# The odd keys' copy on another DMA queue in two parts, a new order of key tiles, and a higher floor of filler products

## The chip, the cores and the metric

The kernel runs on one core of one Trainium2 chip. The metric is the device time of one launch in microseconds (us). The kernel before was run five times: 739.42, 739.61, 740.66, 749.91 and 750.74 us, with a median of 740.66 us. One more execution was recorded by the hardware profiler, and all durations below come from it.

The engines are named as the profile names them: PE (TensorE, matmuls; PEld are its weight loads), DVE (VectorE), ACT (ScalarE), POOL (GpSimd) and SP (SyncE, which here only issues DMAs).

## The reference

The result is a gated sum of two branches that read the same 2048 x 512 input `x`. Branch A is attention with 32 query heads of 16 elements and a single key and value head. Branch B is a gated MLP with a spatial product over the 2048 positions.

```
g = sigmoid(sum(x * gate_w))                      # one gate per position
q = x @ wq -> 32 heads x 2048 x 16 ; k = x @ wk ; v = x @ wv   # k, v: 2048 x 16
a = softmax(q k^T / 4) v  -> 2048 x 512, then @ wo
z = gelu(x @ w_in) ; z1, z2 = halves (688 columns each) ; z2 = layernorm(z2)
b = (z1 * (w_sp @ z2 + b_sp)) @ w_out
out = g * a + (1 - g) * b
```

The scores are 32 x 2048 x 2048 numbers, and each goes through an exponential. That is most of the work.

## The kernel before

**Tiles.** The scores are cut into 32 units. A unit is one of four stretches of 512 queries and one of eight slots; each slot holds four heads, one in each of the four 32-row groups of PE. Odd and even units share a query tile: rows 0 to 15 of a 32-row group belong to the even unit's head and rows 16 to 31 to the odd one's. The key tile `KA` therefore exists twice. `KA[:, 0]` has the keys in the even rows, written by DVE from a PE result (the keys' evacuation, L355), one copy for each of the four stretches of 512 keys. `KA[:, 1]` has the same keys in the odd rows; it is filled by four DMAs from `KA[:, 0]`, one for each row group (`k_shift`, L357), because the move goes from one partition to another. Before the change these four are issued by POOL once all four stretches of keys are there.

A unit has 16 key tiles (128 keys each) by 4 row groups, which makes 64 blocks of 128 x 512 scores. The order in which a unit takes its key tiles is the list `KL` (L35). ACT takes blocks from the front of the list, two to an instruction: an exponential from two PSUM banks to the buffer `P` (L631). DVE takes key tiles from the back of the list, at most seven in a unit, as batches of four blocks. It replaces the exponential by the square of a squared linear term: an instruction on 1024 columns for each pair of blocks (L655), a square over 2048 (L667), and a last square, a part of which goes to POOL (L667 and L674). What the polynomial leaves out is corrected for each unit by two more products with the tables `MC` and `CC`, built once from the keys (`Kt`) and values of the last seven entries of `KL` (`g_MC`, L455). `Kt` holds those keys, repeated, one column block for each key tile. In the old list the last seven entries are all the third or fourth key tile of their stretch, and `Kt` keeps exactly those two of each stretch.

PE makes the scores (`s_mm`, L618), the products of weights and values ("P,V" and "X,V" in the profile), and, between them, everything else: keys, values, queries, branch B and the output projections. At the start a queue of groups has to go in order (L756): values of stretch 0, keys 1, keys 2, values 1, keys 3, values 2, values 3, the correction tables and so on. They share one PSUM bank, `BM`.

**The planner.** The order of instructions on each engine is not written by hand. While the program is built, a list scheduler plays PE, ACT and DVE against a table of assumed durations, and appends an instruction to an engine's program whenever that engine is free and a candidate is ready. On the chip each engine then runs its own list in order and waits on semaphores. What is due to be ready is kept in a table `T`. `T["K1"]` (L367) is the time from which odd units may start; before the change it is the planned end of the last keys' evacuation plus 4500 ns. No score of an odd unit, for ACT or for DVE, is planned before that. A DVE batch of the unit in progress is opened only while the unit has at least 32 blocks left between the two ends (L811).

**Unread products.** `keep_pick` (L1057) adds matmuls that nobody reads. The planner sums the planned load of PE over the last 3400 ns, where a matmul over the full 128 x 128 array and 512 columns counts as 1, so that a score or value product with a 32-row or 32-column tile counts as 0.25. If the sum is below `KEEP` a filler is offered: ones times ones into `BM` when that bank is idle, or zeros added to the bank of running sums `BO` when all four sums of a unit are open. While the sum is also below `LOW`, its priority is 1.5, ahead of value products (2) and of the groups for `BM` (3); between `LOW` and `KEEP` it is 9, behind all that is ready. A candidate that would end past the deadline for the next pair of score blocks for ACT is dropped, fillers included.

**The queues.** SP issues, in this order: the four transposing loads of `x`, the loads of `w_in` (two), `b_sp`, `wo`, `w_out` (three), then four transposing loads of the first quarter of `w_sp` (`ld_wT(0)`, L304). Later quarters and the outputs follow on the same queue. ACT issues the small loads and `wq` before its first activation.

The expression of `keep_pick` that decides:

```
have = sum(w_ for _, w_ in load)
if have >= KEEP or st_["pu"] >= NU:
    return None
...
return (now, 1.5 if have < LOW else 9, C512 + sw("M"), emit, None, "M")
```

Of the kernel before, what the change touches and what calls it, by code (L numbers as in the profile page):

```python
# [15 lines left out]
S = 2048  # L16
D = 512
DH = 16
# [13 lines left out]
ZMAX = 25.0  # L32


KL = (0, 1, 2, 4, 5, 8, 9, 12, 13, 6, 10, 14, 15, 11, 7, 3)  # L35

NPB = 21
NX = 6
# [2 lines left out]
NMAX = 7  # L41
# [16 lines left out]
SLATE = 535.0  # L58
FREE = 60.0
SEEN = 204.0  # L60
KEEP = 7.5
LOW = 6.5
MMARG = 120.0
PMARG = 200.0
PRE = 12
# [107 lines left out]
def build_kernel(nc, x_d, wq_d, wk_d, wv_d, wo_d, win_d, wsp_d, bsp_d, wout_d, gw_d, out_d):  # L173
    es = ExitStack()
    with es:
# [24 lines left out]
        KA = sb("KA", [128, 2, S], B16)  # L200
        QA = sb("QA", [128, NQ, 512], B16)
        V1 = sb("V1", [128, NKT, 32], B16)
        KT0 = sb("KT0", [128, NKT, DH], B16)
        Kt = sb("Kt", [128, 8, 128], B16)
# [18 lines left out]
        ones = sb("ones", [128, 512], B16)  # L223
# [30 lines left out]
        op = pg.op  # L254
# [18 lines left out]
        def dma(eng, fn, r=(), w=(), n=16, tag="", after=()):  # L273
            return op(eng, fn, r=r, w=w, dma=n, tag=tag, after=after)
# [23 lines left out]
        def ld_wT(tc):  # L298
            prev = []
            for k in range(4):  # L300
                r0 = 512 * tc + 128 * k
                prev = [dma("sp", lambda q, r0=r0, k=k: q.dma_start_transpose(wT[:, :, 128 * k:128 * k + 128], wsp_d[r0:r0 + 128, :]),
                            w=[("wT", k)], tag="wT", after=prev)]
        ld_wT(0)  # L304

        for g in range(4):
            op("dve", lambda v, g=g: v.tensor_scalar(wk_rep[:, :, 32 * g:32 * g + 16], wk_sb[:], 0.25, None, ALU.mult), r=["wk"], w=["wk_rep"])
# [38 lines left out]
        def setT(k):  # L346
            def f(t):
                T[k] = t
            return f
# [4 lines left out]
        def k_ev(c, b):  # L354
            op("dve", lambda v: v.tensor_copy(KA[:, 0, 512 * c:512 * c + 512], bank(b)), r=[bkey(b)], w=[("K", 0, c)], tag="Kev")  # L355

        def k_shift():  # L357
            for g in range(4):
                dma("pool", lambda q, g=g: q.dma_start(KA[32 * g + 16:32 * g + 32, 1, :], KA[32 * g:32 * g + 16, 0, :]),
                    r=[("K", 0, c) for c in range(4)] + ["KA1"], w=[("K", 1, g)], tag="Ksh")  # L360

        def g_K(c):
            def done(t):
                T[("K", 0, c)] = t
                if c == 3:
                    k_shift()
                    T["K1"] = t + 4500  # L367
            return Group("K%d" % c, [(C512, lambda dt=dt: k_mm(c, dt, BM)) for dt in range(4)], [(600, lambda: k_ev(c, BM))],
                         lambda: when(("x", c)), done)

# [46 lines left out]
        def g_V(c):  # L417
            def piece(k, dt):
                t0 = 512 * c + 128 * k
                return lambda: mm(bank(BM, 33, 64 * k), xT[:, dt, t0:t0 + 128], wvg[:, dt, 0:33], dt == 0, dt == 3,  # L420
                                  ["wv", "gw", "wvk", ("x", c)], [BMK], tag="V")
            src = bank(BM, 256).rearrange("p (k w) -> p k w", w=64)
            e1 = lambda: op("dve", lambda v: v.tensor_copy(V1[:, 4 * c:4 * c + 4, 0:DH], src[:, :, 0:DH]), r=[BMK], w=[("V", c)], tag="Vev")
            e2 = lambda: op("dve", lambda v: v.tensor_copy(gs[:, 4 * c:4 * c + 4].unsqueeze(2), src[:, :, 32:33]), r=[BMK], w=[("gs", c)], tag="gsev")
            e3 = lambda: op("dve", lambda v: v.tensor_copy(KT0[:, 4 * c:4 * c + 4, :], src[:, :, 16:32]), r=[BMK], w=[("KT0", c)], tag="ktev")

            def done(t):
                T[("V", c)] = t
                dve_q.append((330, lambda: op("dve", lambda v: v.tensor_copy(
                    Kt[:, 2 * c:2 * c + 2, :].rearrange("p k (h d) -> p k h d", d=DH),  # L430
                    KT0[:, 4 * c + 2:4 * c + 4, :].unsqueeze(2).broadcast_to([128, 2, 8, DH])), r=[("KT0", c)], w=[("Kt", c)], tag="Kt"), t, setT(("Kt", c))))
                if c == 3:
                    gate_and_k()
            def all_():
                for k in range(4):
                    for dt in range(4):
                        piece(k, dt)()
            return Group("V%d" % c, [(480, all_)], [(150, e1), (100, e2), (130, e3)],
                         lambda: when(("x", c), "wvg"), done)
# [15 lines left out]
        def g_MC():  # L455
            pieces = []
            for h in range(2):
                for i in range(NMAX):
                    kt = KL[15 - i]
                    pieces.append((90, lambda h=h, i=i, kt=kt: mm(  # L460
                        bank(BM, 32 * (NMAX - i), 256 * h + 32 * i).rearrange("p (n e) -> p n e", e=32),
                        Kt[:, 2 * (kt // 4) + kt % 2, :] if h == 0 else ones[:, 0:128], V1[:, kt, :].unsqueeze(1).broadcast_to([128, NMAX - i, 32]),
                        i == 0, i == NMAX - 1, [("Kt", kt // 4), ("V", kt // 4), "ones"], [BMK], tag="MC")))
            msrc = bank(BM, 32 * NMAX).rearrange("p (n e) -> p n e", e=32).unsqueeze(2).broadcast_to([128, NMAX, 8, 32])
            mk = mke[:].unsqueeze(1).unsqueeze(3).broadcast_to([128, NMAX, 8, 32])
            e1 = lambda: op("dve", lambda v: v.tensor_tensor(MC[:], msrc, mk, ALU.mult), r=[BMK, "mke"], w=["MC"], tag="MC")  # L466
            e2 = lambda: op("dve", lambda v: v.tensor_scalar(ct[:, 0, :], bank(BM, 32 * NMAX, 256), E0, None, ALU.mult), r=[BMK], w=["ct0"], tag="CC")
            cc = CC[:, :, :].rearrange("p n e -> p (n e)")
            e3 = lambda: op("dve", lambda v: v.tensor_copy(cc, ct[:, 0, :]), r=["ct0"], w=["CC"], tag="CC")
            e4 = lambda: op("dve", lambda v: v.tensor_tensor(ct[:, 1, :], ct[:, 0, :], cc, ALU.subtract), r=["ct0", "CC"], w=["ct1"], tag="CC")  # L470
            e5 = lambda: op("dve", lambda v: v.tensor_scalar(ct[:, 1, :], ct[:, 1, :], s01[:, 1:2], None, ALU.mult), r=["ct1", "s01"], w=["ct1"], tag="CC")
            e6 = lambda: op("dve", lambda v: v.scalar_tensor_tensor(cc, cc, s01[:, 0:1], ct[:, 1, :], ALU.mult, ALU.add), r=["CC", "ct1", "s01"], w=["CC"], tag="CC")
            def some(h):
                for c_, f_ in pieces[NMAX * h:NMAX * h + NMAX]:
                    f_()
            return Group("MC", [(500, lambda: some(0)), (500, lambda: some(1))], [(1950, e1), (320, e2), (320, e3), (320, e4), (250, e5), (320, e6)],
                         lambda: when(*[(k, c) for k in ("Kt", "V") for c in range(4)]), setT("MC"))
# [140 lines left out]
        def s_mm(b, blk):  # L618
            u, kt, g = blk
            par = u % 2  # L620
            rk = [("K", 0, kt // 4)] if par == 0 else [("K", 1, g)]
            mm(bank(b), KA[32 * g:32 * g + 32, par, 128 * kt:128 * kt + 128], QA[32 * g:32 * g + 32, (u // 2) % NQ, :], True, True,
               rk + [("Q", (u // 2) % NQ)], [bkey(b)], tp=(32 * g, 0), tag="S")

# [870 lines left out]
```

## Time and profile before

| quantity | value |
|---|---|
| median of five runs | 740.66 us |
| the profiled execution's own time | 742.81 us |
| its span, first to last instruction | 741.0 us |
| ACT busy | 718.4 us (97%), of it 691.9 us in 752 exponentials |
| DVE busy | 713.4 us (96%) |
| PE busy | 677.3 us (91%) |
| POOL busy | 303.1 us (41%) |
| mean granted PE clock over the span | 0.993 |
| fillers, counted by their weight loads | 64 "ones" (12 of them the opening warm-up) and 54 "ones,zeros" |

The profiled execution lasts 1.8 us longer than its span. PE's busy time is that of pipelined matmuls with modelled ends: matmuls that each last 385 ns begin about 215 ns apart, so PE has more room than 91% suggests. In a timeline, a row merges neighbouring instructions of one kind; its first two numbers are the start and the length, and the brackets at its end give the idle time before it and what ended that. In a table of stretches, "PEclk" is the share of the full clock that PE was granted.

### The profile page before, as it was taken

To read this page: it belongs to the slowest core of one execution; us is meant where nothing else is said; L and a number is where in the kernel's file an instruction comes from. 1 tells how busy PE (TensorE), PEld (TensorE's weight loads), DVE (VectorE), ACT (ScalarE), POOL (GpSimd) and SP (SyncE) were. 2 spreads that over 40 slices of the span, in tenths; PEclk is the share of its full clock that TensorE was granted. 3 is DMA by queue.
4 is the path that set the end of the run, shared out by engine and by line. 5 is a ranking of instruction groups with operands and counts; after the bars stand their busy time and mean duration, and the time that the engine had idled before them with its cause. 6 is when DMAs were issued, how large, how long until landed. Compare 5 with 4: busy or idle time off the path is not lost.

```text
span 741.0 us, 14027 instructions
## 1 busy us (share of the span) xinstructions
PE 677.3 (91%) x5439; PEld 192.5 (26%) x5529; DVE 713.4 (96%) x821; ACT 718.4 (97%) x781; POOL 303.1 (41%) x304
## 2 busy tenths in 40 slices
PE   8889989989899999989999999999998999999895
PEld 2322222223222222222222322222222222223221
DVE  7799999999999999999999999999999999999995
ACT  5899999999999999999999999999999999999994
POOL 4234443441444444444244444434554333334440
PEclk9899999999999999999999999999999999999998
DMA  9810000000000000500000150000004000000001
GB/s 202 188 30 1 1 1 1 1 1 1 1 1 1 1 1 17 107 15 8 1 1 1 10 114 15 8 1 1 1 23 93 15 15 1 1 1 1 1 1 33
DMA packets 49114, 17.06 MB, mean 23 GB/s; under 512 B 44145, under 2 KB 48977, under 8 KB 49042
## 3 DMA queue, kind: packets, MB, share of 16 engines
q1 hardware_dynamic: 45986, 15.02, 9.3%
q10 hardware_dynamic: 2928, 0.82, 0.5%
q8 instruction: 45, 0.74, 0.4%
q0 software_dynamic: 128, 0.26, 0.2%
q14 instruction: 27, 0.22, 0.1%
HBM read 3.25 MB, written 2.10 MB: 7 GB/s over the span
## 4 chain that ended last, share of the span: by engine, by line
ACT 57%; issue 18%; PE 18%; DVE 6%; POOL 1%; ACTq 0%
ACT P L631 55%; PE ps L313 12%; PE ps L312 6%; DVE X L655 2%; DVE X L667 1%; ACT z L521 1%; ACT z L529 1%; POOL rc L691 0%; DVE KA L355 0%; DVE MC L466 0%; POOL Tn L697 0%; ACTq L161 0%; DVE T L685 0%; DVE OT L700 0%; ACT L631 0%
## 5 line engine op out<-in xcount | busy, mean ns | idle before, releaser
L631 ACT ACTIVATE P<-ps 128x1024 bf16<-128x1024 f32 x752 | 691.9, 1116 | 4.5 <-PE ps L313 4.0
L313 PE MATMUL ps<-QA,KA 32*128 32x512 bf16 x2048 | 318.6, 385 | 43.1 <-ACT P L631 34.2
L655 DVE TENSOR_SCALAR X<-ps 128x1024 f16<-128x1024 f32 x272 | 330.0, 1213 | 8.3 <-PE ps L313 7.1
L674 POOL TENSOR_TENSOR X<-X 128x416 bf16<-128x416 f16 x189 | 166.1, 879 | 346.2 <-DVE X L667 254.4
L667 DVE TENSOR_TENSOR X<-X 128x2048 f16<-128x2048 f16 (+3 forms) x272 | 291.2, 1076 | 2.0
L313 PEld LDWEIGHTS ps<-QA,KA 32*128 32x128 bf16 x2048 | 78.1, 91 | 320.1 <-ACT P L631 291.6
L313 PE MATMUL ps<-P,V 128*32 128x512 bf16 x1504 | 137.6, 386 | 1.0 <-issue 1.0
L691 POOL TENSOR_TENSOR rc<-T,mone 128x16 f32<-128x16 f32 x31 | 94.7, 3056 | 52.6 <-DVE T L685 52.5
L312 PE MATMUL ps<-wT,z 128*128 128x512 bf16 x286 | 91.0, 384 | 3.8 <-issue 3.8
L313 PE MATMUL ps<-X,V 128*32 128x512 bf16 x544 | 66.8, 386 | 1.0 <-issue 0.8
L313 PEld LDWEIGHTS ps<-P,V 128*32 128x32 bf16 x1504 | 28.5, 94 | 43.5 <-issue 42.9
L312 PEld LDWEIGHTS ps<-wT,z 128*128 128x128 bf16 x320 | 22.5, 97 | 47.6 <-issue 43.2
L312 PE MATMUL ps<-win,xT 128*128 128x344 bf16 x128 | 29.6, 314 | 0.5 <-issue 0.3
L312 PE MATMUL ps<-wout,z 128*128 128x512 bf16 x84 | 26.6, 384 | 1.9 <-issue 1.1
L685 DVE STREAM_TRANSPOSE T<-ps 128x512 f32<-128x512 f32 x32 | 22.7, 710 | 1.6 <-PE ps L313 1.6
L697 POOL TENSOR_TENSOR Tn<-T,rcg 128x256 bf16<-128x256 f32 x31 | 21.3, 686 | 2.4
L312 PE MATMUL ps<-wo,OT 128*128 128x512 bf16 x58 | 19.7, 385 | 2.1 <-DVE OT L700 1.8
L312 PE MATMUL ps<-ones 128*128 128x512 bf16 x55 | 19.4, 439 | 1.8 <-DVE ones L256 1.5
L313 PEld LDWEIGHTS ps<-X,V 128*32 128x32 bf16 x544 | 15.6, 94 | 17.5 <-issue 15.5
L312 PE MATMUL ps<-xT,win 128*128 128x512 bf16 x78 | 18.2, 380 | 1.0 <-ACT z L521 0.7
L312 PE MATMUL ps<-xT,wq 128*128 128x512 bf16 x58 | 17.9, 384 | 0.3 <-DVE X L655 0.2
L512 DVE CAST z<-ps 128x344 bf16<-128x344 f32 x32 | 16.2, 506 | 0.3
(113 smaller groups left out, 288.6 us busy)
## 6 DMA issues: line engine op xcount, KB each, us to landing
out_dram<-outsb SPq DMA_DIRECT2D x14, 128.0 KB, 1.7
win<-in_B_w_in_dram SPq DMA_DIRECT2D x2, 688.0 KB, 5.5
wout<-in_B_w_out_dram SPq DMA_DIRECT2D x1, 640.0 KB, 9.0
wo<-in_A_wo_dram SPq DMA_DIRECT2D x1, 512.0 KB, 6.5
wq<-in_A_wq_dram ACTq DMA_DIRECT2D x1, 384.0 KB, 5.5
wT<-in_B_w_sp_dram SPq DMA_TRANSPOSE x16, 4.5
KA<-KA POOLq DMA_DIRECT2D x4, 64.0 KB, 2.9
out_dram<-outsb ACTq DMA_DIRECT2D x2, 128.0 KB, 3.2
```

The lines of the kernel that those rows point to most:

```text
L312: return t.matmul(dst, lhsT, rhs, start=start, stop=stop)
L313: return t.matmul(dst, lhsT, rhs, start=start, stop=stop, tile_position=tp)
L512: ev = lambda: op("dve", lambda v: v.tensor_copy(z2[:, FH * st + 344 * h:FH * st + 344 * h + 344], bank(BM, 344)), r=[BMK], w=[("z2", st)] ...
L521: op("act", lambda a: a.activation(z1[:, 1024 * i:1024 * i + 1024], bank(b, 1024), ACT.Gelu_apprx_tanh), r=[bkey(b), bkey(b + 1)], w=[("z1 ...
L529: op("act", lambda a: a.activation(z, z, ACT.Gelu_apprx_tanh), r=[("z2", st) for st in sts], w=[("z2", st) for st in sts], tag="gelu2")
L631: op("act", lambda a: a.activation(P[:, 512 * p:512 * (p + n)], ps[:, 512 * b0:512 * (b0 + n)], ACT.Exp), r=[bkey(b0 + i) for i in range(n ...
L655: op("dve", lambda v: v.tensor_scalar(X[:, m % NX, 1024 * h:1024 * h + 1024], bank(BD, 1024), PA, PB, ALU.mult, ALU.add), r=[bkey(BD), bke ...
L667: op(eng, lambda v: v.tensor_tensor(x if tag == "dU" else x.bitcast(B16), x, x, ALU.mult), r=ks, w=ks, tag=tag)
L674: op("pool", lambda g: g.tensor_tensor(x.bitcast(B16), x, x, ALU.mult), r=ks, w=ks, after=[pg.ops["dve"][-1]], tag="gW")
L685: o("dve", lambda v: v.transpose(T1[:], bank(BO)), r=[("bk", BO)], w=["T1"], tag="T1")
L691: o("pool", lambda g: g.tensor_tensor(rc[:].unsqueeze(2), lsum, mone[:].unsqueeze(2), ALU.pow), r=["T1", "mone"], w=["rc"], tag="rc")
L697: o(e, lambda v: v.tensor_tensor(tn, t1[:, :, 0:16], s_[:].unsqueeze(2).broadcast_to([128, 16, 16]), ALU.mult), r=["T1", k], w=[("Tn", pr, ...
```

## The change

Five things change together.

1. `KL` becomes 0, 1, 2, 4, 5, 6, 8, 9, 10, 12, 13, 14, 15, 11, 7, 3. The last four entries stay 15, 11, 7, 3; the last seven are now 12, 13, 14, 15, 11, 7, 3.
2. `Kt` follows: the fourth key tile of stretches 0 to 2 and all four of stretch 3, so the four DVE copies that fill it have 1, 1, 1 and 4 tiles instead of 2 each. `g_MC` reads the new places.
3. The copy of keys to the odd rows is issued by SP instead of POOL, and in two parts of four DMAs: keys 0 to 1535 once stretches 0 to 2 are evacuated, keys 1536 to 2047 after stretch 3. A score of an odd unit waits for the part that its key tile lies in. `T["K1"]` becomes the planned end of the last keys' evacuation plus 5000 ns.
4. The first quarter of `w_sp` is issued by SP after the second part of that copy, and not before it.
5. `KEEP` goes from 7.5 to 8.0 and `LOW` from 6.5 to 7.0.

```diff
-KL = (0, 1, 2, 4, 5, 8, 9, 12, 13, 6, 10, 14, 15, 11, 7, 3)
+KL = (0, 1, 2, 4, 5, 6, 8, 9, 10, 12, 13, 14, 15, 11, 7, 3)
...
-KEEP = 7.5
-LOW = 6.5
+KEEP = 8.0
+LOW = 7.0
...
-        ld_wT(0)
...
-        def k_shift():
+        def k_shift(z):
+            lo, hi = ((0, 1536), (1536, S))[z]
             for g in range(4):
-                dma("pool", lambda q, g=g: q.dma_start(KA[32 * g + 16:32 * g + 32, 1, :], KA[32 * g:32 * g + 16, 0, :]),
-                    r=[("K", 0, c) for c in range(4)] + ["KA1"], w=[("K", 1, g)], tag="Ksh")
+                dma("sp", lambda q, g=g: q.dma_start(KA[32 * g + 16:32 * g + 32, 1, lo:hi], KA[32 * g:32 * g + 16, 0, lo:hi]),
+                    r=[("K", 0, c) for c in (range(3) if z == 0 else (3,))] + ["KA1"], w=[("K", 1, g, z)], tag="Ksh")
...
                 T[("K", 0, c)] = t
+                if c == 2:
+                    k_shift(0)
                 if c == 3:
-                    k_shift()
-                    T["K1"] = t + 4500
+                    k_shift(1)
+                    ld_wT(0)
+                    T["K1"] = t + 5000
...
-                dve_q.append((330, lambda: op("dve", lambda v: v.tensor_copy(
-                    Kt[:, 2 * c:2 * c + 2, :].rearrange("p k (h d) -> p k h d", d=DH),
-                    KT0[:, 4 * c + 2:4 * c + 4, :].unsqueeze(2).broadcast_to([128, 2, 8, DH])), ...
+                n, k0 = (1, 4 + c) if c < 3 else (4, 0)
+                dve_q.append((66 + 134 * n, lambda: op("dve", lambda v: v.tensor_copy(
+                    Kt[:, k0:k0 + n, :].rearrange("p k (h d) -> p k h d", d=DH),
+                    KT0[:, 4 * c + 4 - n:4 * c + 4, :].unsqueeze(2).broadcast_to([128, n, 8, DH])), ...
...
-                        Kt[:, 2 * (kt // 4) + kt % 2, :] if h == 0 else ones[:, 0:128], ...
+                        Kt[:, kt - 12 if kt > 11 else 4 + kt // 4, :] if h == 0 else ones[:, 0:128], ...
...
-            rk = [("K", 0, kt // 4)] if par == 0 else [("K", 1, g)]
+            rk = [("K", 0, kt // 4)] if par == 0 else [("K", 1, g, kt // 12)]
```

More of the change, by code (lines that the diff above doesn't have):

```diff
@@ L428, in done @@
                 T[("V", c)] = t
-                dve_q.append((330, lambda: op("dve", lambda v: v.tensor_copy(
-                    Kt[:, 2 * c:2 * c + 2, :].rearrange("p k (h d) -> p k h d", d=DH),
-                    KT0[:, 4 * c + 2:4 * c + 4, :].unsqueeze(2).broadcast_to([128, 2, 8, DH])), r=[("KT0", c)], w=[("Kt", c)], tag="Kt"), t, setT(("Kt", c))))
+                n, k0 = (1, 4 + c) if c < 3 else (4, 0)
+                dve_q.append((66 + 134 * n, lambda: op("dve", lambda v: v.tensor_copy(
+                    Kt[:, k0:k0 + n, :].rearrange("p k (h d) -> p k h d", d=DH),
+                    KT0[:, 4 * c + 4 - n:4 * c + 4, :].unsqueeze(2).broadcast_to([128, n, 8, DH])), r=[("KT0", c)], w=[("Kt", c)], tag="Kt"), t, setT(("Kt", c))))
                 if c == 3:
@@ L461, in g_MC @@
                         bank(BM, 32 * (NMAX - i), 256 * h + 32 * i).rearrange("p (n e) -> p n e", e=32),
-                        Kt[:, 2 * (kt // 4) + kt % 2, :] if h == 0 else ones[:, 0:128], V1[:, kt, :].unsqueeze(1).broadcast_to([128, NMAX - i, 32]),
+                        Kt[:, kt - 12 if kt > 11 else 4 + kt // 4, :] if h == 0 else ones[:, 0:128], V1[:, kt, :].unsqueeze(1).broadcast_to([128, NMAX - i, 32]),
                         i == 0, i == NMAX - 1, [("Kt", kt // 4), ("V", kt // 4), "ones"], [BMK], tag="MC")))
```

## The prediction, made before the result was known

> **What bounds the kernel.** I read the busy shares first, then the table of stretches, the waits, and the timelines of the stretch that stood out. ACT (718.4 of 741.0 us) and DVE (713.4) are full together; they divide the 2048 score blocks between them, 1504 to 544, so neither alone is the bound. From 42 us on ACT has almost no gap. Its gaps lie between 23 and 40 us, in one place of the start:
>
> ```profile
> 23.18:28.40 5.22, 3.38 (x46) 1.44 (x45) 4.31 (x12) 3.78 (x6) 2.33 (x5) 0.88 0.94 150
> 28.40:34.20 5.80, 5.80 (x44) 2.23 (x42) 2.95 (x9) 4.18 (x5) 0.87 (x1) 0.52 0.55 111
> ...
> 60.00:160.00 100.00, 89.78 (x752) 26.13 (x758) 99.45 (x117) 100.00 (x110) 42.99 (x42) 1.00 0.01 1
> ...
> 192.00:729.00 537.00, 502.27 (x4073) 136.41 (x4142) 527.18 (x549) 536.57 (x585) 232.60 (x223) 1.00 0.07 16
> ```
>
> The columns are the stretch, its length, busy time (and instructions) of PE, PEld, DVE, ACT and POOL, the granted PE clock, the DMA share and GB/s. In the second row PE is busy throughout while its clock is 0.52: PE holds ACT to 4.18 of 5.80 us and DVE to 2.95. The later stretches show ACT at 100 of 100 and 536.57 of 537. ACT's timeline names the gaps:
>
> ```profile
> 9.78 13.40 ACT L631 ACTIVATE P<-ps 128x1024 bf16<-128x1024 f32 x14 [0.48 <-PE ps L313]
> 24.62 3.77 ACT L631 ACTIVATE P<-ps 128x1024 bf16<-128x1024 f32 x4 [1.44 <-PE ps L313]
> ...
> 30.07 1.02 ACT L631 ACTIVATE P<-ps 128x1024 bf16<-128x1024 f32 x1 [0.49 <-PE ps L313]
> 31.47 1.02 ACT L631 ACTIVATE P<-ps 128x1024 bf16<-128x1024 f32 x1 [0.38 <-PE ps L313]
> 32.99 1.02 ACT L631 ACTIVATE P<-ps 128x1024 bf16<-128x1024 f32 x1 [0.50 <-PE ps L313]
> 34.24 5.77 ACT L631 ACTIVATE P<-ps 128x1024 bf16<-128x1024 f32 x6 [0.23 <-PE ps L313]
> ```
>
> After 14 exponentials ACT waits 1.44 us for scores. Behind that wait, in PE's and DVE's timelines, stand the keys of stretch 3:
>
> ```profile
> 21.95 0.82 PE L312 MATMUL ps<-xT,wk_rep 128*128 128x512 bf16 x3
> 22.61 0.81 PE L312 MATMUL ps<-ones,zeros 128*128 128x512 bf16 x3
> 24.19 0.40 PE L313 MATMUL ps<-QA,KA 32*128 32x512 bf16 x4 [0.78 <-DVE KA L355]
> ```
> ```profile
> 23.45 0.68 DVE L355 CAST KA<-ps 128x512 bf16<-128x512 f32 x1
> ...
> 31.51 1.23 DVE L655 TENSOR_SCALAR X<-ps 128x1024 f16<-128x1024 f32 x1 [1.88 <-PE ps L313]
> ```
>
> The old list asks for key tile 12 as its eighth entry, after 7 x 4 blocks, which are those 14 exponentials; its keys are there at 23.45 + 0.68 = 24.13 us.
>
> **The order of key tiles.** The new list needs stretch 3 only at its tenth entry, after 9 x 4 blocks, 18 exponentials. At 13.40 / 14 = 0.957 us each, exponential 19 is due at 9.78 + 18 x 0.957 = 27.0 us, 2.9 us behind the keys. Stretch 2 is needed from exponential 13 (21.3 us) and is evacuated at 17.16 + 0.68 = 17.84; stretch 1 as before. So the 1.44 us go, unless the new plan makes the keys of stretch 3 more than 2.9 us later.
>
> **The clock.** With 0.77 in 26 to 28 us, 0.50 to 32 and 0.52 in 32 to 34, PE ran at half clock for 0.92 + 4.0 + 1.92 = 6.84 us. Just before, between 24.0 and 27.4 us, PE issued 4 + 2 + 2 score products (2.0 in the planner's units), 16 + 16 small value products (at 33 of 512 columns each, 2.1) and 2 fillers: about 6. Elsewhere stretches of 3.4 us mostly come to 8 and more, all at 1.00. The change raises the floor by 0.5, takes out the wait in which PE stood still, and puts score products in its place. I take it that the light stretch goes, with ACT's 0.49 + 0.38 + 0.50 + 0.23 = 1.60 us and DVE's 1.88 us at 31.51. Bounds: nothing is saved if the stretch stays light; at most all of this.
>
> [...]
>
> **Unread products.** There are 52 + 54 = 106 fillers after the warm-up. If PE were always at its floor, 0.5 more per 3.4 us over 714 us would add 105; as most stretches are above 8, I take 50, an estimate, with 0 and 105 as ends. One takes about 0.21 us ((0.81 - 0.39) / 2 in the row of three above), so 10 us of PE, at most 22. The cover is the time in which PE's next score weights wait for ACT, which a filler off the deadline fills:
>
> ```profile
> PEld ps L313 <- ACT P L631: 291.6, 686, 1.0
> ```
>
> I take nothing from the end for them; uncovered, they cost up to 22 us.
>
> **The copy of keys.** POOL loses four issues (2.15 us at 24.44); it is at 41% and its next piece waited for DVE, so nothing is gained there.
>
> ```profile
> 24.44 2.15 POOL L359 DMA_DIRECT2D KA<-KA  x4 [1.08 <-DVE KA L355]
> ...
> 15.44 0.61 SPq L294 DMA_DIRECT2D wout<-in_B_w_out_dram  x1
> 16.09 1.27 SPq L295 DMA_DIRECT2D wout<-in_B_w_out_dram  x1
> 17.41 0.48 SPq L296 DMA_DIRECT2D wout<-in_B_w_out_dram  x1
> 17.93 20.35 SPq L302 DMA_TRANSPOSE wT<-in_B_w_sp_dram  x4
> ```
>
> On POOL the copy landed 2.8 to 3.0 us after its issue, by about 29.5 us. On SP eight issues at about 0.5 us: the first four from 17.9, behind weights that took 9.0 us (`w_out`, issued at 15.44) and 7.4 us (its last piece, 17.41) to land, so by some 25 us; the last four from 24.2 to 26.2, landing by 29.1 (at the old 2.9) or at the worst 35.2 (at 9.0). Moving the transposes of `w_sp` behind it keeps their 20.35 us of issue out of the way, and their first reader, the spatial product, starts at 207 us, so the 8 us that they come later cost nothing. The first odd unit begins with key tiles of the first part (0 from ACT, 3 from DVE), and DVE's first odd pair stood at 30.8 us. I take no wait. What does cost is the planned 5000 instead of 4500 ns: DVE's first odd batch is planned 0.5 us later, in a stretch in which DVE has nothing else.
>
> [...]
>
> **Copies to `Kt`.** Four of 225 ns (0.9 us) become three of one tile and one of four. The same 8 tiles become 7; I take no change, within 0.2 us either way.
>
> **The sum.** ACT gets 1.44 + 1.60 = 3.04 us, which at 0.93 us for two blocks (43 in 40.13 us in its last stretch) are 6.5 blocks. DVE gets 1.88 - 0.5 = 1.38 us, at 544 blocks in 713 us some 1.1 blocks. The two together do 2.15 + 0.76 = 2.91 blocks a us, so the end comes 7.6 / 2.91 = 2.6 us earlier. From the profiled 742.81 that is 740.2; the median of the runs lies 2.15 us under the profiled execution, so **738.0 us**.
>
> **Rivals.** (1) The light stretch stays or moves, so the fillers don't do what they are for: only the 1.44 us are saved, 3.1 blocks or 1.1 us, less DVE's half us: 739.7. For it: `BM` is taken by groups in a row there and fillers need a free bank. (2) Fillers come ahead of scores: they cannot be broken off, and at priority 1.5 they go before value products. Each on the path costs 0.21 us; 12 of them use up the gain, 48 make it slower by 1%, and half of the 105 (11 us) give 742.81 - 2.6 + 11 - 2.15 = 749. Against it: the 291.6 us above, and the drop at the deadline. (3) SP's queue delivers late: from 30.8 to 35.2 us PE would stand before an odd score with everything behind it in its list, 4.4 us, giving 742.4. (4) A newly laid plan also mends what stays open here (0.78 and 0.68 us of DVE, ACT's 4.50 us before its last instructions): 4.5 + 2.6 us, 733, and a little more if the two engines divide their last unit better: 732.
>
> **How the numbers follow.** Forecast 0.40; rival (1) 0.24; (2) 0.15; (3) 0.10; (4) 0.11. Every edit lays the plan anew, which I cannot work out by hand; it spreads each case by a few us. The range goes from case (4) to case (2), 732 to 749, leaving out what is beyond these. One per cent is 7.4 us, about what a measurement of this kernel can tell from no change: faster by more than that needs more than case (4) and some luck, 0.11; slower by more needs 48 uncovered fillers, or more than one new dip of the clock at some 2 to 3 us each, 0.16; in between 0.73.
>
> **What would show it.** Right: no ACT gap over 0.5 us before 40 us; granted clock 1.00 from 24 to 36 us; the copy's last DMA landed before 30 us; 130 to 180 fillers; ACT still at 100% from 60 to 160 us. Wrong: half clock at another place, new waits of ACT for PE after 42 us, PE standing before an odd score at 29 to 35 us, or a longer end in which ACT and DVE don't finish together.

## The result, and the profile after

Over 28 executions the changed kernel takes 738.54 us in the median (737.02 to 749.88), against 742.86 us (739.42 to 750.74, 54 executions) for the kernel before beside it: a ratio of 0.9946, interval 0.9929 to 0.9964. The forecast of 738.0 us and its class, within 1%, came out. Most of its working did not.

Executions of one kernel differ by up to 12 us, and the time goes with the mean granted PE clock of the execution. Over all comparisons of this study the clock of 104 executions of the kernel before is on record: their median is 741.59 us, their mean 742.86, and a time is about 0.53 us longer (a straight line through the 104) for each 0.001 less of mean clock. As 0.001 of 740 us is 1.48 us at half clock (0.50), one us at half clock costs about 0.36 us, an estimate from that line. Where the executions have to be told apart, "at full clock" below means a mean clock of at least 0.996: 44 of those 104, with a median of 739.92 us. Of the changed kernel 22 of the 31 with a recorded clock, the profiled one among them, are at full clock, with a median of 738.34 us. So the gain has two parts: 1.6 us at full clock, and the rest from more executions at full clock (the chance of shares as far apart as 22 of 31 and 44 of 104, were they equal, is under 1%).

The profiled execution of the changed kernel was an unlucky one: its own time is 744.92 us, its span 743.1, its mean clock 0.984. It is slower than the profiled one of before (742.81) although the kernel is faster. Two stretches at half clock account for that, by the estimate below the table. The table of stretches, changed kernel; the columns are those of the prediction (stretch, length, busy time and instructions of PE, PEld, DVE, ACT and POOL, granted PE clock, DMA share, GB/s):

```profile
9.00:24.00 15.00, 13.60 (x93) 3.33 (x89) 11.18 (x21) 11.32 (x12) 0.91 (x2) 0.66 1.09 278
24.00:36.00 12.00, 10.95 (x118) 4.33 (x119) 10.22 (x29) 12.00 (x15) 2.63 (x3) 1.00 0.27 61
...
60.00:160.00 100.00, 91.80 (x757) 26.81 (x769) 98.28 (x117) 99.58 (x110) 43.17 (x42) 1.00 0.00 1
...
180.00:200.00 20.00, 17.50 (x110) 5.38 (x110) 16.57 (x33) 17.37 (x19) 4.25 (x2) 0.74 0.00 1
200.00:729.00 529.00, 496.70 (x4032) 135.56 (x4100) 521.27 (x541) 528.94 (x577) 225.19 (x222) 1.00 0.07 16
```

Half clock was granted from 12.1 to 22.4 us and from 189.6 to 199.9 us (0.50 over each). A score product took 603 ns in the mean from 12.5 to 22 us and 384 ns from 24 to 36 us. The row from 24 to 36 us, where before had the dip, is at 1.00, with ACT busy for all of its 12 us. From 60 us on ACT is full outside the second dip (99.58 of 100 us, 528.94 of 529), as it was. By the slope above, from the 0.9975 that executions at full clock have on average to 0.984 are 13.5 x 0.53 = 7.2 us; on top of 738.34 they give 745.5, and 744.92 was measured: by this estimate, whose slope is that of the kernel before, the clock accounts for the whole of this execution's lag.

ACT's timeline of the start, changed kernel (start, length, line, tile, count, in brackets the idle time before and what ended it):

```profile
17.82 2.11 ACT L636 ACTIVATE P<-ps 128x1024 bf16<-128x1024 f32 x2 [1.03 <-PE ps L312]
20.42 2.10 ACT L636 ACTIVATE P<-ps 128x1024 bf16<-128x1024 f32 x2 [0.48 <-PE ps L312]
22.80 10.19 ACT L636 ACTIVATE P<-ps 128x1024 bf16<-128x1024 f32 x11 [0.28 <-PE ps L312]
32.86 28.11 ACT L636 ACTIVATE P<-ps 128x1024 bf16<-128x1024 f32 x30
```

Its gaps of 1.03, 0.48 and 0.28 us lie in the new dip and just behind it, and PE ended each. The old gap of 1.44 us is gone; a trace without the dip (experiment 3) shows that more plainly.

SP's timeline, changed kernel, and the wait that the prediction gave as the fillers' cover:

```profile
21.67 8.84 SPq L360 DMA_DIRECT2D KA<-KA  x8
30.56 16.86 SPq L302 DMA_TRANSPOSE wT<-in_B_w_sp_dram  x4
```

```profile
PEld ps L312 <- ACT P L636: 274.2, 655, 1.0
```

The eight issues of the copy stand behind the weights and ahead of the four transposes, as written. The cover went from 291.6 to 274.2 us.

### The profile page after: what moved, and what is told of

It is laid out like the page before. It is cut to its first block, busy times and chain, and to the rows that moved or that the text cites. A ratio compares the mean times of both kernels' runs of the same rounds, so it can differ in the third digit from the quotient of the medians.

```text
span 743.1 us, 14068 instructions
## 1 busy us (share of the span) xinstructions
PE 686.1 (92%) x5458; PEld 194.0 (26%) x5550; DVE 711.9 (96%) x821; ACT 719.3 (97%) x781; POOL 295.6 (40%) x299
## 4 chain that ended last, share of the span: by engine, by line
ACT 56%; issue 19%; PE 17%; DVE 5%; POOL 2%; ACTq 0%; POOLq 0%
ACT P L636 56%; PE ps L312 10%; PE ps L311 7%; DVE X L660 2%; DVE X L672 1%; POOL rc L696 0%; DVE z L517 0%; DVE T L690 0%; DVE MC L471 0%; POOL bspz L264 0%; POOL KA L261 0%; ACTq L161 0%; DVE OT L705 0%; ACT L636 0%; DVE QA L389 0%
## 5 line engine op out<-in xcount | busy, mean ns | idle before, releaser
L312 PE MATMUL ps<-P,V 128*32 128x512 bf16 x1504 | 141.1, 388 | 0.8 <-issue 0.8
L696 POOL TENSOR_TENSOR rc<-T,mone 128x16 f32<-128x16 f32 x31 | 92.2, 2973 | 48.8 <-DVE T L690 48.8
L312 PE MATMUL ps<-X,V 128*32 128x512 bf16 x544 | 68.8, 388 | 0.4 <-issue 0.3
L311 PE MATMUL ps<-ones 128*128 128x512 bf16 x63 | 23.2, 443 | 2.2 <-DVE ones L256 1.4
L702 POOL TENSOR_TENSOR Tn<-T,rcg 128x256 bf16<-128x256 f32 x31 | 19.2, 620 | 2.4
L311 PE MATMUL ps<-ones,zeros 128*128 128x512 bf16 x49 | 18.2, 392 | 0.3 <-issue 0.3
```

The costliest lines, as they stand in the source:

```text
L311: return t.matmul(dst, lhsT, rhs, start=start, stop=stop)
L312: return t.matmul(dst, lhsT, rhs, start=start, stop=stop, tile_position=tp)
L696: o("pool", lambda g: g.tensor_tensor(rc[:].unsqueeze(2), lsum, mone[:].unsqueeze(2), ALU.pow), r=["T1", "mone"], w=["rc"], tag="rc")
L702: o(e, lambda v: v.tensor_tensor(tn, t1[:, :, 0:16], s_[:].unsqueeze(2).broadcast_to([128, 16, 16]), ALU.mult), r=["T1", k], w=[("Tn", pr, ...
```

## Experiments

All twelve in one table. "Full" is the number of executions at full clock and their median.

| kernel | differs by | median (range, n) | ratio to before, interval | full: share, median | mean time |
|---|---|---|---|---|---|
| before | | 741.59 (738.36-751.17, 104) | | 44/104, 739.92 | 742.86 |
| changed | | 738.57 (737.02-749.88, 31) | 0.9946, 0.9929-0.9964 | 22/31, 738.34 | 739.69 |
| 1 e1_floor | before + floor 8.0 | 743.89 (740.68-747.81, 12) | 1.0013, 0.9974-1.0053 | 6/12, 741.19 | 743.91 |
| 2 e2_nofloor | changed, floor 7.5 | 736.76 (736.09-740.10, 12) | 0.9922, 0.9889-0.9955 | 8/12, 736.58 | 737.37 |
| 3 e3_pool | changed, copy by POOL | 738.55 (737.84-746.20, 12) | 0.9964, 0.9935-0.9992 | 9/12, 738.48 | 739.16 |
| 4 e4_short | changed, narrow fillers | 772.43 (771.32-774.47, 6) | 1.0393, 1.0335-1.0451 | 0/6 | 772.75 |
| 5 e5_list | before + new list | 741.25 (738.83-749.54, 12) | 1.0010, 0.9972-1.0048 | 3/12, 739.30 | 742.51 |
| 6 e6_sp | before + copy by SP, 5000 ns | 739.82 (738.53-746.36, 12) | 0.9984, 0.9950-1.0017 | 7/12, 739.32 | 741.06 |
| 7 e7_high | changed, floor 8.5 | 739.48 (738.99-742.45, 12) | 0.9962, 0.9934-0.9989 | 10/12, 739.38 | 739.70 |
| 8 e8_lowfloor | changed, floor 7.0 | 740.63 (737.36-743.73, 12) | 0.9960, 0.9923-0.9997 | 1/12, 737.36 | 740.46 |
| 9 e9_sp45 | no. 2, 4500 ns | 740.84 (738.40-742.85, 12) | 0.9946, 0.9914-0.9979 | 5/12, 739.07 | 740.59 |
| 10 e10_pool50 | no. 2, copy by POOL | 737.34 (736.28-744.89, 7) | 0.9899, 0.9845-0.9954 | 4/7, 736.69 | 738.26 |
| 11 e11_waits | no. 2 + fillers at waits | 737.40 (736.17-737.78, 12) | 0.9923, 0.9890-0.9956 | 12/12, 737.39 | 737.21 |
| 12 e12_before_waits | before + fillers at waits | 741.63 (739.57-751.13, 13) | 0.9981, 0.9951-1.0010 | 7/13, 740.11 | 742.38 |

Numbers 1 to 4 ran together on one chip, 5 to 8 on one, 9 to 11 on one, and 12 later on that of 1 to 4. The kernel before, run beside each group, has 739.65, 739.86, 740.06 and 740.04 us at full clock, so a comparison across groups is good to about 0.4 us. The times at full clock of one kernel scatter by 0.3 to 0.7 us (standard deviation), the means of twelve by 0.2 to 1.0 us (standard error), so differences between kernels are read at full clock first. The shares at full clock are counts out of 6 to 31 executions, so a few more or less are chance.

### 1 and 2. The floor alone, and the change without it

```diff
 # 1: before                     # 2: changed kernel
-KEEP = 7.5                     -KEEP = 8.0
-LOW = 6.5                      -LOW = 7.0
+KEEP = 8.0                     +KEEP = 7.5
+LOW = 7.0                      +LOW = 6.5
```

> The kernel before with only KEEP 8.0 and LOW 7.0 (148 fillers instead of 106; order of key tiles and copy on POOL as before). Theory A (fillers: what is gained is a granted clock that stays up): the fastest run stays at 739 to 740 us, but the median falls by 2 to 3 us, to about 740, and the mean clock of the runs rises from about 0.993 to 0.997. Theory B (order: what is gained is ACT's 1.44 us wait for the keys of stretch 3): median within 0.7 us of the kernel before. Theory C (fillers stand in the way of scores): slower than before, about 0.2 us for each of the 42 that is on the path.

> The changed kernel with KEEP 7.5 and LOW 6.5 again (115 fillers instead of 127): everything but the higher floor. Theory A: the fastest run keeps the changed kernel's 737 us, the median rises by 2 us or more, to above 740.5, with a lower mean clock. Theory B: median 738 to 739, all of the gain is here.

The higher floor on the old kernel adds 42 fillers (148 for 106) and gains nothing: 739.92 to 741.19 us at full clock, and no more executions at full clock (6 of 12; 13 of the 29 of before beside it). Taken out of the changed kernel (115 fillers for 127) it gives back 738.34 - 736.58 = 1.8 us, and 8 of 12 stay at full clock against 22 of 31. So this part costs something and buys nothing that these counts can show. Number 1's plan also gives DVE one batch of four blocks less (754 exponentials on ACT instead of 752), which has a price of its own (see number 9); its 1.3 us are therefore not the price of fillers alone. Number 2's 736.76 us are faster than either of its two theories had it. The profile of experiment 1 shows something else. PE's timeline, number 1:

```profile
30.30 0.60 PE L313 MATMUL ps<-QA,KA 32*128 32x512 bf16 x3
31.95 0.39 PE L313 MATMUL ps<-QA,KA 32*128 32x512 bf16 x1 [1.04 <-DMA KA<-KA]
```

PE stands 1.04 us in the middle of the first odd scores for the POOL copy, one DMA of which took 5.9 us from issue to landing (2.6 in the median of the four). In the profile of before all four took 2.8 to 3.0 us, so that the last had landed by 28.9 us, ahead of the first odd scores; the prediction had read "no wait" from that.

### 3. The changed kernel with the copy back on POOL

```diff
-                dma("sp", ... KA[..., 1, lo:hi], KA[..., 0, lo:hi] ...)   # two parts
+                dma("pool", ... KA[..., 1, :], KA[..., 0, :] ...)         # whole rows
...
-                    k_shift(1)
-                    ld_wT(0)          # and ahead of the copy again
+                    k_shift()
                     T["K1"] = t + 5000
```

> The changed kernel with the copy of keys issued by POOL in one part and the first quarter of w_sp ahead of it, as before; the orders of PE, ACT and DVE are those of the changed kernel, instruction by instruction. If the queue of the copy is worth nothing (forecast): within 0.7 us of the changed kernel's 738.5. If the move to SP is what gains: slower by 1.5 us or more, with PE standing before the first odd scores at about 30 us.

PE, ACT and DVE run the same orders as in the changed kernel. 738.48 against 738.34 us at full clock: with 5000 ns planned the queue is worth nothing that can be told, as the forecast had it. Its profile is the clean picture of the new order that the changed kernel's own could not give. Stretches and ACT's timeline, number 3:

```profile
9.00:24.00 15.00, 13.56 (x118) 4.08 (x112) 14.52 (x28) 14.10 (x16) 2.67 (x4) 1.00 1.17 280
24.00:36.00 12.00, 11.61 (x130) 4.58 (x130) 10.07 (x26) 12.00 (x15) 3.02 (x5) 1.00 0.72 105
```

```profile
11.71 17.75 ACT L633 ACTIVATE P<-ps 128x1024 bf16<-128x1024 f32 x19 [0.58 <-PE ps L314]
29.27 30.91 ACT L633 ACTIVATE P<-ps 128x1024 bf16<-128x1024 f32 x33
```

19 exponentials in 17.75 us, then 33 more, and no gap between. With the same order on PE as in the changed kernel, half clock is in neither place at which that trace had it: the clock is 1.00 from 9 to 24 us and from 180 to 200 us.

### 4. Narrow fillers

```diff
-                    mm(bank(BO), zeros[:], ones[:], ...)
+                    mm(bank(BO, 32), zeros[:], ones[:, 0:32], ...)
...
-                mm(bank(b), ones[:, 0:128], ones[:], ...)
+                mm(bank(b, 32), ones[:, 0:128], ones[:, 0:32], ...)
```

> The changed kernel with each of its 127 fillers cut from 512 to 32 columns, the order of all engines unchanged. Theory A: the granted clock falls to half in several stretches, and the median rises by 4 to 15 us, with a mean clock of 0.95 to 0.99. Theory C: PE gets 127 x 0.2 = 25 us of room and the median falls by 1 to 3 us. Fillers that do nothing: within 0.7 us.

The order and the number of fillers are those of the changed kernel, each 32 columns wide instead of 512. Stretches, number 4:

```profile
12.00:64.00 52.00, 51.90 (x323) 13.19 (x323) 38.25 (x61) 40.28 (x43) 10.33 (x10) 0.51 0.42 106
64.00:196.00 132.00, 121.19 (x971) 38.39 (x969) 128.06 (x171) 131.44 (x142) 48.56 (x48) 1.00 0.00 1
196.00:232.00 36.00, 33.20 (x182) 6.79 (x182) 28.15 (x44) 29.34 (x31) 11.95 (x10) 0.53 0.00 1
564.00:771.00 207.00, 188.72 (x1437) 48.06 (x1435) 184.05 (x194) 186.33 (x202) 77.39 (x78) 0.88 0.06 16
```

772.4 us: 127 unread products carry 34 us, where the theory that had the sign (A) expected 4 to 15. In the first row the clock does not go with the profile's idle time: for 52 us PE counts as busy for 51.90 us, and its clock is 0.51, with ACT at 40.28 of 52. PE ran 323 products there, 6.2 a us, and 7.4 a us (971 in 132 us) in the next row at 1.00. What brought the clock back at 64 us is not shown.

### 5 and 6. The list alone, and the SP copy alone

```diff
 # 5: before                                  # 6: changed kernel
-KL = (0, 1, 2, 4, 5, 8, 9, 12, ...)         -KL = (0, 1, 2, 4, 5, 6, 8, 9, ...)
+KL = (0, 1, 2, 4, 5, 6, 8, 9, ...)          +KL = (0, 1, 2, 4, 5, 8, 9, 12, ...)
 # and Kt's layout with it                    # and Kt's old layout; KEEP 7.5, LOW 6.5
```

> The kernel before with only the new list of key tiles and its places in the tables (copy on POOL, planned 4500 ns, KEEP 7.5 and LOW 6.5; 105 fillers). The theory that stands after the first four runs: the list is the gain. Then this is 2 to 5 us faster than the kernel before, 736.5 to 739 us, ACT's 1.44 us gap at 23 us is gone, and a run at full clock takes about 737 us against 739.5. Rival (the gain of the run without the higher floor, 736.8 us, comes from the planned 5000 ns or the copy in two parts): within 0.7 us of the kernel before.

> The kernel before with only the copy on SP in two parts, the first quarter of w_sp behind it, and the planned 5000 ns; the orders of PE, ACT and DVE come out as those of the kernel before, instruction by instruction. List theory: within 0.7 us of the kernel before at the same granted clock. If the copy's queue matters: 1 us or more faster, since at full clock the first odd scores could start before POOL's copy lands at 29.5 us; or slower by up to 4.4 us, if SP delivers it behind the weights.

The list alone gains nothing in the median (ratio 1.001), where the theory expected 2 to 5 us, and 0.6 us at full clock. PE's timeline shows a new wait, and the view of the tile `KA` gives the sum of such waits (us, times; PE's 1.86 us and its weight load's wait for the same copy are both in it), number 5:

```profile
29.68 0.39 PE L313 MATMUL ps<-QA,KA 32*128 32x512 bf16 x3 [0.19 <-ACT P L632]
31.93 0.39 PE L313 MATMUL ps<-QA,KA 32*128 32x512 bf16 x1 [1.86 <-DMA KA<-KA]
```

```profile
  DMA KA<-KA: 4.0, 2
...
DMA to landing us min/median/max: 2.4/2.6/5.2
```

ACT no longer waits at 24 us, and PE waits at 30 us, for a slow one of the four POOL copies. That this wait ate the list's gain is tested by number 9.

Number 6 has the instruction orders of before on PE, ACT and DVE, although 5000 ns are planned; only the copy (queue and two parts) and the place of the first quarter of `w_sp` behind it differ. Its ACT timeline:

```profile
24.55 3.77 ACT L635 ACTIVATE P<-ps 128x1024 bf16<-128x1024 f32 x4 [1.44 <-PE ps L312]
28.29 32.61 ACT L635 ACTIVATE P<-ps 128x1024 bf16<-128x1024 f32 x35
```

The old list's gap of 1.44 us is there again and nothing after it: PE waits for no DMA at the odd scores. At full clock that is worth 739.92 - 739.32 = 0.6 us, within the 0.7 us of the list theory; in the mean 1.3 us (742.39 for the 35 executions of before beside it, to 741.06; standard errors 0.6 and 0.8), which chance could give.

### 7 and 8. Other floors

```diff
 # 7: changed kernel         # 8: changed kernel
-KEEP = 8.0                 -KEEP = 8.0
-LOW = 7.0                  -LOW = 7.0
+KEEP = 8.5                 +KEEP = 7.0
+LOW = 7.5                  +LOW = 6.0
```

> The changed kernel with KEEP 8.5 and LOW 7.5 (169 fillers instead of 127). If each step of the floor costs a little of PE's time on the path and buys no clock (theory after the first four runs): 739.5 to 742 us at full clock, median not below the changed kernel's 738.5. If the floor buys clock: fewer runs under a mean clock of 0.996, median 738 or less.

> The changed kernel with KEEP 7.0 and LOW 6.0 (74 fillers instead of 127). If the floor of 7.5 is already near what keeps the clock up: at full clock 735.5 to 736.5 us, but more half-clock stretches, median 738 to 745 us with a mean clock under 0.99. If fillers only cost: 735 to 736 us in the median.

With 7.0 (74 fillers) one execution of twelve keeps the clock (mean clock 0.990); with 7.5 eight of twelve, with 8.0 22 of 31, with 8.5 (169 fillers) ten of twelve. Among these four plans the floor seems to matter below 7.5, and above it the counts don't tell the settings apart. But each floor was tried with one plan, and other plans at 7.5 have 3 of 12 (number 5) and 5 of 12 (number 9). At full clock 8.5 costs 739.38 - 736.58 = 2.8 us against 7.5; part of that is another plan with 754 exponentials on ACT, as the next pair shows.

### 9 and 10. 4500 against 5000 ns, and the queue, at the lower floor

```diff
 # 9: number 2                          # 10: number 2, copy as in number 3
-                    T["K1"] = t + 5000
+                    T["K1"] = t + 4500
```

> The list-only kernel with the copy on SP in two parts and the first quarter of w_sp behind it; planned time still 4500 ns, KEEP 7.5 and LOW 6.5; the orders of PE, ACT and DVE are those of the list-only kernel, instruction by instruction. There PE stood 4.0 us before odd scores until POOL's copy landed. If that wait is what ate the list's gain: the wait is gone or under 0.5 us, and the median falls from 741.2 to 737 to 739 us. If the plan of 4500 ns is bad in itself: within 0.7 us of the list-only kernel.

> The list-only kernel with the planned time at 5000 ns, the copy still on POOL in one part; the orders of PE, ACT and DVE are those of the changed kernel without its higher floor, instruction by instruction. If the landing of the copy decides: the odd scores stand half a microsecond later, so the wait shrinks to under 1 us, and the median lies between 736.8 (copy on SP) and 739 us. If SP's queue is needed for the gain: 740 us or more. At the higher floor the same exchange cost nothing (738.55 against 738.54).

Number 9 has the orders of number 5, with the copy on SP: 739.07 against 739.30 us at full clock, and 1.9 us in the mean (742.51 to 740.59, standard errors 1.0 and 0.4). PE no longer waits for the copy, and yet the median, 740.84 us, stays within 0.7 us of number 5's 741.25, as the second theory had it: the wait is not what ate the list's gain. Number 10 has the orders of number 2: 736.69 against 736.58. So the queue is worth 0.2 to 0.6 us at full clock with the orders of numbers 5 and 6, with a lean to 1.3 to 1.9 us in the mean, and nothing with the orders of number 2 or of the changed kernel.

The half microsecond itself, which the prediction had priced as a loss, gains 739.07 - 736.58 = 2.5 us at full clock from number 9 to number 2, and 2.4 to number 10, which ran beside number 9. It does so with the new list only; with the old one it leaves the plan as it is (number 6). The groups of instructions and the DVE timeline at the end, first number 9, then number 2:

```profile
L636 ACT ACTIVATE P<-ps 128x1024 bf16<-128x1024 f32 x754 | 692.6, 1123 | 0.8 <-PE ps L312 0.5
```

```profile
727.55 0.72 DVE L690 STREAM_TRANSPOSE T<-ps 128x512 f32<-128x512 f32 x1 [6.04 <-PE ps L312]
```

```profile
L636 ACT ACTIVATE P<-ps 128x1024 bf16<-128x1024 f32 x752 | 691.3, 1124 | 4.1 <-PE ps L312 3.8
```

```profile
728.49 0.72 DVE L690 STREAM_TRANSPOSE T<-ps 128x512 f32<-128x512 f32 x1 [2.17 <-PE ps L312]
```

The kernel before, with its 752 exponentials, at the same place:

```profile
730.75 0.72 DVE L685 STREAM_TRANSPOSE T<-ps 128x512 f32<-128x512 f32 x1 [1.08 <-PE ps L313]
```

With 4500 ns and the new list, DVE takes one batch of four blocks less over the whole kernel; ACT does 754 exponentials instead of 752, and DVE stands 6.04 us before the last transpose while ACT ends its unit. With 5000 ns it stands 2.17 us. So the half microsecond gives back a batch that the new list loses at 4500 ns. Numbers 1, 5, 7 and 9 are the plans with 754. (Number 2 was profiled with a dip of its own, 0.66 from 9 to 24 us, so the absolute times of its rows are late.) Two exponentials at about 0.92 us are 1.8 of the 2.5 us, an estimate. DVE's share moves in steps of a batch, and half a microsecond at 30 us decides which way it falls. That the step is what makes the gain was read from the traces, not varied by itself.

Numbers 6 and 2 differ in the list and `Kt`'s layout alone, both with 5000 ns: there the list is worth 739.32 - 736.58 = 2.7 us at full clock. With 4500 ns (number 9, against number 6 with the orders of before) it is worth 0.25.

### 11 and 12. Fillers where PE really waits

The changed kernel's trace shows PE waiting in the 5 us before its second dip, which may be why the clock still falls. PE's timeline there:

```profile
184.80 0.39 PE L312 MATMUL ps<-QA,KA 32*128 32x512 bf16 x2 [0.58 <-ACT z L526]
185.35 1.24 PE L311 MATMUL ps<-ones 128*128 128x512 bf16 x5 [0.16 <-issue]
187.13 0.39 PE L312 MATMUL ps<-QA,KA 32*128 32x512 bf16 x2 [0.55 <-ACT P L636]
...
188.97 0.39 PE L312 MATMUL ps<-QA,KA 32*128 32x512 bf16 x2 [0.53 <-ACT P L636]
```

PE's order is fixed. A filler behind a score that waits for ACT waits with it (the five products of ones at 185.35 us begin behind the two scores that stood 0.58 us), and the planner, which goes by planned times, sees no gap there. Number 11 puts nine more fillers ahead of the scores that wait, outside the planner's count:

```diff
+        def extra(n):
+            for _ in range(n):
+                mm(bank(BM), ones[:, 0:128], ones[:], ...)
+                load.pop()
...
+                if c == 0:                       # ahead of the first values' products
+                    extra(3)
...
+                        if st_["nz"] in (3, 4, 6) ...:   # score pairs after the z1 phase
+                            extra(2)
```

> The changed kernel without its higher floor (KEEP 7.5, LOW 6.5), with 9 unplanned fillers put where PE stood idle in the traces: 3 ahead of the first values' products at about 10 us, 2 each ahead of three of the first score pairs after the first half of branch B (about 176 us). All planned orders as without them. If the half-clock stretches come from real waits that a floor over planned load does not see: no run under a mean clock of 0.994 (4 of 12 without these fillers were at 0.995 or less), median 736 to 736.8 us. If they come from elsewhere: the same share of runs under 0.995, median 736.5 to 737.5 us.

All 12 executions are at full clock, against 12 of 19 of numbers 2 and 10 (the chance of such a difference, were the shares equal, is about 3%), and the spread shrinks to 736.17 to 737.78 us. That is the sign named for the theory of real waits; the median, 737.40 us, lies in the range named for the other. The price is 737.39 - 736.58 = 0.8 us at full clock, so the median is no better than number 2's; the mean is about the same too (737.21 and 737.37).

Number 12 does the same to the old kernel: three fillers ahead of the first values, three and two zeros-products ahead of the scores of key tiles 12 and 13 of the first unit, where ACT has its gap, and two each ahead of the second, third and sixth score pair after the first half of branch B.

```diff
+                        if bl[0][0] == 0 and bl[0][1] == 12:
+                            extra0(3 if bl[0][2] == 0 else 0)
+                        if bl[0][0] == 0 and bl[0][1] == 13 and bl[0][2] == 0:
+                            extra0(2)
```

> The kernel before with 14 unplanned fillers where PE stood idle in its trace: 3 ahead of the first values' products, 3 ahead of the scores that wait for the keys of stretch 3 and 2 just after, 2 each ahead of three of the first score pairs after the first half of branch B. All planned orders as in the kernel before. If the half-clock stretches of the kernel before come from these waits, they, and not the list, are the larger part of the change's gain in the median: at least 10 of 12 runs at a mean clock of 0.996 or more (36 of 87 without), median 739.5 to 740.5 us, as its undisturbed runs have it. If they come from other places: half of the runs or fewer at 0.996, median above 741.

It missed: 7 of 13 at full clock, 8 of 17 for before beside it. So what worked in number 11 did not in the old kernel, and what makes the clock fall there stays open. PE's timeline and the stretches, number 12:

```profile
29.62 0.39 PE L313 MATMUL ps<-QA,KA 32*128 32x512 bf16 x3
...
32.25 0.39 PE L313 MATMUL ps<-QA,KA 32*128 32x512 bf16 x1 [2.24 <-DMA KA<-KA]
```

```profile
24.00:33.00 9.00, 6.08 (x77) 2.56 (x76) 5.02 (x18) 6.62 (x8) 3.02 (x5) 1.00 0.70 122
33.00:48.00 15.00, 14.53 (x94) 3.28 (x91) 11.50 (x17) 11.02 (x11) 3.01 (x2) 0.55 0.34 72
```

The clock held through the row up to 33 us; PE came about 1 us earlier to the first odd score than in the profile of before, stood 2.24 us for the POOL copy, and lost the clock behind it. Number 5's trace has the same sequence (a wait of 1.86 us, then 0.62 from 33 to 42 us). Number 1's has a wait of 1.04 us at the same place and no half clock until 201 us, so the wait alone does not decide. In the profile of before there was nothing to wait for: its last copy had landed by 28.9 us, ahead even of number 12's first odd score at 29.62.

## Why the total was right and the terms were not

**The order of key tiles: the gap right, its worth not.** ACT's 1.44 us are gone in the clean trace of number 3, and the keys of stretch 3 cause no new gap. The 1.1 us worked out for it were not met either way. With 4500 ns the list moved the time by 0.25 us (6 to 9) to 0.6 us (before to 5) at full clock, as its plan leaves DVE a batch short; with 5000 ns by 2.7 us (6 to 2). Number 9 rules out that the wait for the copy took the difference. What makes 2.7 us out of a gap of 1.44 us is not shown.

**The copy: this step failed.** "Nothing is gained there" and "I take no wait" came from one execution in which all four copies landed in 2.8 to 3.0 us. In three other traces one of the four took 5.2 to 5.9 us, and PE stood 1.04, 1.86 and 2.24 us at the first odd scores. With SP PE waited for no copy in seven traces (the changed kernel, numbers 2, 6 to 9 and 11). Priced at full clock the queue gives 0.2 to 0.6 us; the lean to 1.3 and 1.9 us in the mean, in the two pairs of equal orders, is 1.4 to 1.7 standard errors. How often the slow landing occurs without the profiler is not known.

**Rival (3), SP late: the delay is real and harmless.** In five traces (numbers 6 to 9 and 11) the eight copies begin just behind the weights, at 18.1 to 19.4 us; the slowest took 6.6 to 7.4 us to land, the quickest 1.7 to 1.9. In the changed kernel's own the four issued from 21.7 to 23.6 us took 2.8 to 4.0 us, the four from 28.1 us on 1.7 to 1.9. What makes the difference is not shown. All were there in time.

**5000 instead of 4500 ns: wrong sign.** Forecast as 0.5 us of DVE lost; measured as 2.5 us gained with the new list (number 9 to 2), and as no change of plan with the old one. The prediction judged it in its place at 30 us; as far as the traces tell, it acted through DVE's batch, at the end.

**The clock: the right subject, the wrong cause.** The terms of 1.60 and 1.88 us took the dip for a fixed piece of the program, which the higher floor would mend. It comes and goes between executions, and it moves: 44 of 104 executions of before are at full clock, and the changed kernel had it elsewhere in its profiled execution. A light stretch does not bring it every time: counted as the prediction counts, from the weight loads, the 3.4 us from 23.0 us on come to 4.5 in the profile of before, but those from 193.0 (5.5) and from 414.0 us (6.0), as light as its "about 6", stayed at full clock (1.00). The floor from 7.5 to 8.0 changed neither plan's share beyond the counts' noise. The share did go from 42% to 71%. Number 2, without the floor, is already at 8 of 12, which points to the other parts, though counts of twelve don't prove it. In two of the three traces with a wait for the copy the clock fell just behind it, in the third it did not; and number 9, with no such wait, is at 5 of 12. What decides stays open.

**The fillers' cost: not nothing.** 1.8 us (number 2 to the changed kernel) and 1.8 (10 to 3) at full clock, and 1.3 (before to number 1) together with a lost batch of DVE, where the prediction took nothing against its cover. Rival (2) had the sign and a size too large. Only 21 came (127 for 106), not 50. As each floor also lays a new plan, it is open how much of this is fillers on the path.

**The sum.** At full clock, in steps: SP copy -0.6 (before to number 6), new list -0.25 (6 to 9; with the old list 4500 and 5000 give the same plan), 5000 ns -2.5 (9 to 2), floor +1.8 (2 to changed): -1.6 us. The rest of the median's gain is executions that keep the clock. 2.6 us were forecast, from ACT's gap and the dip. Two large terms that the forecast lacked, the step of a batch and the floor's price, partly cancel. The total also stands on a median of 740.66 us from five executions; 54 executions of the same kernel have 742.86. So the change gained 4.3 us in the median and not 2.6, and it started 2.2 us higher: two errors of about 2 us nearly cancel in 738.0, and the hit in the total is luck to that extent. Rival (4), a plan that happens to mend more, is nearest to number 2: 736.8 us, against its 733.

**The signs named.** In the changed kernel's own trace the clock from 24 to 36 us was 1.00, as named, and ACT was busy for 99.58 of the 100 us from 60 on. But ACT had a gap of 1.03 us, there were 127 fillers and not 130 or more, the last copy landed at 31.8 us and not before 30, and half clock stood at another place, which had been named as a sign of being wrong.

**The copies to `Kt`: right.** Three of 0.18 to 0.20 us and one of 0.29 make 0.87 us, for 0.9.

Numbers 2, 10 and 11 beat both kernels. Number 2 is the changed kernel with the old floor: 736.76 us. Number 11 has the narrowest range.

## What to carry to other kernels

Before a stall is called free or gone, look for the wait that stands right behind it, and test whether that wait is worth anything; a single trace shows one landing time and one place of the clock's dip. Take the baseline from many executions when one kernel scatters by 12 us. Change the parts of a bundle one at a time, and also together: here a part meant to help cost 1.8 us, and the list and the half microsecond gained 2.7 us together, where the one alone gained 0.25 to 0.6 and the other nothing. To hold the clock, try unread work ahead of the instruction that waits; all 12 executions were at full clock in number 11, and only 7 of 13 in number 12. A floor on planned load can't see a wait that the plan doesn't have.

## What the runs showed of the hardware that was not expected

- Half clock with PE busy 51.90 of 52 us (number 4): with narrow fillers PE was busy by the profile's count and the clock was 0.51. 127 products, some 27 us of PE at 0.21 us each, are worth 34 us here.
- A us at half clock costs about 0.36 us of the end in this kernel, which ACT and DVE bound: an estimate from the slope over 104 executions, 0.53 us for each 0.001 of mean clock.
- The same instruction order had half clock at 12.1 to 22.4 and 189.6 to 199.9 us in one execution (changed kernel) and in neither place in another (number 3, 1.00 from 9 to 24 and from 180 to 200 us).
- Four equal copies within SBUF, issued by POOL within 2.15 us, landed after 2.4 to 5.9 us in one execution (number 12) and after 2.8 to 3.0 in another with the same orders but for the fillers (before); PE went on when the slow one had landed.
